# Row sums in another PSUM ring, one cast on another engine, and weight loads issued later, in a windowed attention kernel with a two-layer feed-forward behind it

## The chip, the cores and the metric

The kernel runs on one core of a Trainium2 chip. The metric is the device time of one execution in microseconds (us). Before the change the median of three runs is 311.28 us (310.89 to 311.34). A difference of less than about 0.2% is not told apart from none.

## What is computed

The reference is attention in a sliding window, followed by a feed-forward with a leaky ReLU. With q, k and v of shape (8 batches, 8 heads, 576 tokens, 64):

```python
scores = scale * np.matmul(q, k.transpose(0, 1, 3, 2))
mask = np.abs(pos[:, None] - pos[None, :]) <= 32
attn = softmax(np.where(mask, scores, -1e9))
x = np.matmul(attn, v)          # then to (4608 tokens, 512)
h = x @ w_in                    # 512 x 2048
out = np.maximum(0.01 * h, h) @ w_out   # 2048 x 512
```

All arrays are float32; the kernel works in bfloat16 with float32 sums.

## The kernel before, in words

**Units of work.** Two heads make a pair, so each batch has four pairs. For the first two batches one *item* is one pair and one half of the 576 tokens (288): items 0 to 3 are the four pairs of the first half of batch 0, items 4 to 7 those of its second half, items 8 to 15 belong to batch 1. Later batches use a different form (`score_blocks`, `product_blocks`, lines 363 to 406), which the change does not touch. "The second and third pairs" of the change are items 1 and 2.

**What an item needs, in order.** q and k of the pair are loaded by SP (`load_qk`, line 68) and v by GpSimd's own DMA queue, which also casts it (`load_cast_v`, line 143). q and k are cast to bfloat16 (`cast_qk`, line 265), transposed on TensorE into a PSUM buffer and copied out by ScalarE (`transposes`, line 306: a generator, of which each `next(first)` does q or k of one pair). Then:

- `score` (408): ten small matmuls into the one score buffer `ps` (419), the exponential on ScalarE (431), the product with the 0/1 mask on GpSimd (433; item 0's on VectorE), which gives `prob`;
- `row_sums` (446): two matmuls of `prob` with a block of ones (454) into PSUM, which spread each row's sum over the partitions;
- `inverse` (460): a reciprocal of these sums on VectorE (462); `sums` (465) does both;
- `product` (470): five matmuls with v into PSUM (477), and `scaled` (489): VectorE multiplies by the reciprocal and writes the item's part of `xT`, the input of the feed-forward.

**The feed-forward.** `xT` is multiplied with `w_in` in tiles of 128 hidden columns (`h_mms` 512, `h_tile` 525, index `f` from 0 to 15), ScalarE applies the leaky ReLU into `gT` (523), and `gT` is multiplied with `w_out` (585, 601). The first four hidden tiles of the first half are opened together by `h_first` (561), which goes through the four 128-row chunks of `xT` (one per pair, so one per item) and does all four tiles of a chunk before the next: four matmuls per `next(h0)`.

**PSUM.** There are eight banks: `ps` takes two, the pool `xps` has one buffer each for the names `s` (row sums) and `x` (products), and the pool `mmps` has four buffers that are handed out in turn to everything with the tag `mm`: the transposes of batch 0, the hidden tiles and the output tiles. Whoever takes a buffer waits until its former reader is done. So with the single buffer `s`, the row sums of an item wait until the reciprocal of the item before has read it.

**Order.** The kernel is scheduled by hand: each engine runs its instructions in the order in which the program issues them. Lines 688 to 750 write out the start (items 0 to 6 and the first hidden tiles); then the loop in line 764 runs the hidden tiles 4 to 15 of the first half, and `second_half` (754) does one more product, row sum and score between them. `warm_up` (610) and `keep_busy` (617) are matmuls without use for the result, with which TensorE is kept at work.

**Queues.** `load_w_in` (673) and `load_w_out` (676) load the weights in four parts each, 512 hidden columns at a time, and cast them; they are issued by GpSimd, between its mask products, and go through the software DMA queue. The q and k loads of batch 1 (line 740) are issued by SP, but a small memset on GpSimd (line 75), placed in GpSimd's order, has to run first. They feed the casts of batch 1 (784, 786, 778, 805), of which the last query cast is the one of pair 3.

**Later.** From group 2 on, a planner (810 to 837) spreads the steps of the other items between hidden and output tiles by due times. The change does not touch it.

Of the kernel before, what the change touches and what calls it, by code (L numbers as in the profile page):

```python
# [9 lines left out]
FP32 = mybir.dt.float32  # L10
# [6 lines left out]
def kernel(  # L17
# [15 lines left out]
    nc = tc.nc  # L33
# [9 lines left out]
    HALF = S // 2  # L43
# [14 lines left out]
    mmps = ctx.enter_context(tc.tile_pool(name="mmps", bufs=4, space=PS))  # L58
    scps = ctx.enter_context(tc.tile_pool(name="scps", bufs=1, space=PS))
    xps = ctx.enter_context(tc.tile_pool(name="xps", bufs=1, space=PS))  # L60
# [7 lines left out]
    def load_qk(b, p, behind=None):  # L68

        for into, src, name in ((qf, q, "qf"), (kf, k, "kf")):
            t = fload.tile([128, 2 * RUN * D], FP32, name=f"{name}{p}")
            if behind is not None:
                behind.memset(t[0:1, 0:1], 0.0)
                behind = None
            heads = src[b, 2 * p:2 * p + 2]
            if b == 0:

                into[b, p] = t[:, 0:NB * D]  # L80
                nc.sync.dma_start(  # L81
                    out=into[b, p], in_=heads.rearrange("a (p c) d -> (a p) (c d)", c=NB))
                continue
            t = t[0:96].rearrange("p (a r) -> p a r", a=2)
            if b < BY_DMA:
                nc.sync.dma_start(out=t, in_=heads.rearrange("a (p c) d -> p a (c d)", c=RUN))
            elif into is qf:
                nc.sync.dma_start(
                    out=t.rearrange("p a (g e) -> p a g e", g=3),
                    in_=heads.rearrange("a (g p c) d -> p a g (c d)", g=3, c=2),  # L90
                )
            else:
                nc.sync.dma_start(
                    out=t.rearrange("p a (c d) -> p a c d", d=D),
                    in_=heads.rearrange("a (c p) d -> p a c d", p=96),
                )
            into[b, p] = t
# [45 lines left out]
    def load_cast_v(b, p, heads=range(2)):  # L143

        for a in heads:
            r = slice(64 * a, 64 * a + 64)
            nc.gpsimd.dma_start(
                out=vbd[b % 2][r, p, :, r],
                in_=v[b, 2 * p + a].rearrange("(c p) d -> p c d", p=64),
            )  # L150
# [114 lines left out]
    def cast_qk(b, p, q_eng=nc.gpsimd, k_eng=nc.gpsimd):  # L265
        for eng, src, dst in ((q_eng, qf, qb), (k_eng, kf, kb)):
            if eng is None:
                continue
            if b == 0:
                to, tok = dst[:, p, 0:NB * D], src[b, p]  # L270
            else:
                to = dst[0:96, p].rearrange("p (c a d) -> p c a d", a=2, d=D)
                tok = src[b, p].rearrange("p a (c d) -> p c a d", d=D)
            if eng is nc.scalar:
                eng.activation(out=to, in_=tok, func=AF.Copy)
            else:
                eng.tensor_copy(out=to, in_=tok)  # L277
# [77 lines left out]
    def where(i):  # L355
        return i // 8, (i // 4) % 2, i % 4
# [6 lines left out]
    def score_blocks(i):  # L363
        p, bs = i % NPAIR, blocks_of(i)
        n = 2 * 64 * len(bs)
        lo = 512 * (i % 2)
        sc = ps[:, lo:lo + n].rearrange("p (a w c i) -> p a w c i", a=2, c=2, i=32)
        for w, (b, m) in enumerate(bs):
            tok = qz[b % 2][:, p, m // 3].rearrange("p a (c i) -> p a c i", c=2)
            at = 32 * (m % 3)  # L370
            nc.tensor.matmul(  # L371
                sc[:, :, w], kz[b % 2][:, p, 64 * m:64 * m + 128],
                tok[:, :, :, at:at + 32], start=True, stop=True,
            )
        e = attn.tile([128, 2 * HALF], BF16, name="e")
        nc.scalar.activation(out=e[:, 0:n], in_=ps[:, lo:lo + n], func=AF.Exp, scale=scale)  # L376
        pr = prob[:, i % NPROB].rearrange("p n i -> p (n i)")[:, 0:n]
        nc.gpsimd.tensor_mul(pr, e[:, 0:n], band.rearrange("p w c i -> p (w c i)")[:, 0:n])  # L378
        probs[i] = pr.rearrange("p (a w i) -> p a w i", a=2, i=64)
# [28 lines left out]
    def score(i, masked_by=nc.gpsimd):  # L408
        if i >= OLD:
            return score_blocks(i)  # L410
        b, hf, p = where(i)
        tok = qT[b][:, p, hf * HALF:hf * HALF + HALF]
        if b == 0:

            for a, n_, m in ((0, 0, 0), (1, 1, 0), (0, 0, 1), (1, 1, 1), (0, 0, 2),
                             (0, 1, 0), (1, 0, 0), (0, 1, 1), (1, 0, 1), (1, 0, 2)):
                blk, i0, n = WIN[hf][n_][m]
                r = slice(64 * a, 64 * a + 64)
                nc.tensor.matmul(  # L419
                    ps_v[r, n_, i0:i0 + n], first_keys[p][r, 64 * blk:64 * blk + 64],  # L420
                    tok[r, i0:i0 + n], start=True, stop=True,
                )
        else:
            for n_, blocks in enumerate(WIN[hf]):
                for blk, i0, n in blocks:
                    nc.tensor.matmul(  # L426
                        ps_v[:, n_, i0:i0 + n], kbd[b % 2][:, p, blk],
                        tok[:, i0:i0 + n], start=True, stop=True,
                    )
        e = attn.tile([128, 2 * HALF], BF16, name="e")  # L430
        nc.scalar.activation(out=e, in_=ps[:, P0:P0 + 2 * HALF], func=AF.Exp, scale=scale)  # L431
        pr = prob[:, i % NPROB]
        masked_by.tensor_mul(  # L433
            pr.rearrange("p n i -> p (n i)"), e, mask[hf].rearrange("p n i -> p (n i)"),
        )
        probs[i] = [pr, None, None]
# [9 lines left out]
    def row_sums(i):  # L446

        pr, both, _ = probs[i]
        s = xps.tile([128, 512], FP32, name="s")[:, 0:HALF]
        if both is not None:  # L450
            nc.tensor.matmul(s, ones_bd, both, start=True, stop=True)
        else:
            for n in range(2):
                nc.tensor.matmul(  # L454
                    s, ones_bd, pr[:, n],
                    start=(n == 0), stop=(n == 1),
                )
        probs[i][2] = s

    def inverse(i):  # L460
        r = recip.tile([128, HALF], FP32, name="r")
        nc.vector.reciprocal(r, probs[i][2])  # L462
        probs[i][2] = r

    def sums(i):
        if probs[i][2] is None:
            row_sums(i)
            inverse(i)
# [20 lines left out]
    def scaled(i):  # L489
        _, x, r = probs.pop(i)  # L490
        nc.vector.tensor_mul(place(i), x, r)  # L491
# [118 lines left out]
    def warm_up(n):  # L610
        t = xps.tile([128, 512], FP32, name="x")
        for _ in range(n):
            nc.tensor.matmul(
                t[:, 0:128], ones_bd, ones_bd, start=True, stop=True, skip_group_check=True,
            )
# [57 lines left out]
    def load_w_in(f0, f1):  # L673
        nc.gpsimd.dma_start(out=w_in_bf[:, :, f0:f1], in_=w_in_r[:, :, f0:f1])

    def load_w_out(i):
        c = slice(4 * i, 4 * i + 4)
        nc.gpsimd.dma_start(out=w_out_bf[:, c, :], in_=w_out_r[:, c, :])

    first = transposes(0)  # L680

    def clear_on_act(t):
        nc.scalar.activation(
            out=t.rearrange("p n j -> p (n j)"),
            in_=zero.to_broadcast([128, NB * 128]), func=AF.Copy,
        )
# [16 lines left out]
    load_cast_v(0, 3, (0,))  # L703
    cast_qk(0, 2, nc.vector, nc.vector)
    score(1)
    sums(0)
    cast_qk(0, 3, None, nc.gpsimd)
    next(first)
    next(first)
    cast_qk(0, 3, nc.scalar, None)  # L710
    warm_up(4)
    load_w_in(512, 1024)
    sums(1)
    score(2)
    load_cast_v(0, 3, (1,))
    load_w_in(1024, 1536)
    next(first)
    next(first)
    product(0)
    scaled(0)  # L720
    score(3)
    sums(2)
    product(1)
    scaled(1)
# [1 line left out]
    score(4)  # L726
    load_w_in(1536, 2048)
    clear_on_act(kbd[1][:, 1])
    load_w_out(0)
    h0 = h_first(0)  # L730
    h = next(h0)
    keep_busy(h, HALF, 3)
# [6 lines left out]
    clear_on_act(kbd[1][:, 2])  # L739
    for p in range(NPAIR):  # L740
        load_qk(1, p, nc.gpsimd if p == 0 else None)
    load_w_out(1)
    row_sums(4)
    product(3)
    scaled(3)
# [8 lines left out]
    def second_half():  # L754

        i = state["done"]
        weighted(i)
        if i < 7:
            sums(i + 1)
        if i < 5:  # L760
            score(i + 3)
        state["done"] += 1

    for f in range(4, FFC):
        h_tile(0, f)
        if f in (4, 8, 12):
            second_half()
        if f == 4:
            load_w_out(3)
            for t in (vbd[1][:, 0], vbd[1][:, 1], kbd[1][:, 3]):  # L770
                nc.gpsimd.memset(t, 0.0)
# [142 lines left out]
```

## Time and profile before

| | |
|---|---|
| median of three runs | 311.28 us (310.89 to 311.34) |
| the profiled execution: its own time, and its span | 311.33 us, 309.6 us |
| TensorE matmuls (PE) | 296.8 us busy, 96% |
| VectorE (DVE) | 223.9 us, 72% |
| ScalarE (ACT) | 203.8 us, 66% |
| GpSimd (POOL) | 200.9 us, 65% |
| matmuls of the first layer, line 515 | 956, 133.1 us |
| matmuls of the second layer, line 585 | 537, 122.5 us |
| row-sum reciprocals, line 462 | 16, 1951 ns each |
| mask products on GpSimd, line 433 | 15, 1297 ns each |

The span runs from the first to the last instruction on the core; the execution's own time is 1.7 us longer. Times in the profile are counted from the start of the span. "PE" is TensorE's matmuls, "PEld" its weight loads, "SPq" SP's DMA issues. A line of the timeline gives start, duration, engine, line of the kernel, operation, output and input, how many instructions were merged, and in brackets how long the engine had been idle and what released it. A line of the chain gives start, duration and the work that the end was waiting for. The profile prints the clock granted to TensorE as 1.00 in every stretch.

### The profile page before, as it was taken

How to read it: one execution, taken by the hardware profiler on the slowest of the kernel's cores; microseconds unless marked ns; L12 is line 12 of the kernel's file. 1: busy time of each engine (PE TensorE's matmuls, PEld its weight loads, DVE VectorE, ACT ScalarE, POOL GpSimd, SP SyncE). 2: the span in 40 equal slices, each digit the busy share in tenths (PEclk: the TensorE clock that was granted, in tenths of full speed). 3: DMA queues.
4: the chain of work that ended last, by engine and by line, in shares of the span. 5: the costliest groups of instructions: out<-in, count | busy, mean ns of one | idle time of the engine just before them, and what ended most of it. 6: DMA issues, size and time to landing. Idle time of an engine off the chain costs nothing.

```text
span 309.6 us, 6903 instructions
## 1 busy us (share of the span) xinstructions
PE 296.8 (96%) x2601; PEld 194.2 (63%) x2630; DVE 223.9 (72%) x300; ACT 203.8 (66%) x421; POOL 200.9 (65%) x254
## 2 busy tenths in 40 slices
PE   2889999999999999999999999999999999999996
PEld 2657865585856768685858585959555555444643
DVE  5778679798879987898799777898679866744000
ACT  6657784482965858585849584849588548842731
POOL 8798699959799997779579357578857522110000
PEclk9999999999999999999999999999999999999999
DMA  7999999997999899999999998895960110001002
GB/s 242 201 153 215 267 215 174 253 177 169 217 217 197 194 240 162 209 151 253 186 172 166 244 224 127 188 206 102 209 129 1 37 68 36 0 34 70 35 27 75
DMA packets 121505, 48.29 MB, mean 156 GB/s; under 512 B 96256, under 2 KB 115968, under 8 KB 121472
## 3 DMA queue, kind: packets, MB, share of 16 engines
q1 hardware_dynamic: 107776, 42.48, 67.2%
q0 software_dynamic: 13696, 5.38, 14.8%
q8 instruction: 20, 0.33, 0.5%
q14 instruction: 13, 0.11, 0.1%
HBM read 36.70 MB, written 9.44 MB: 149 GB/s over the span
## 4 chain that ended last, share of the span: by engine, by line
PE 83%; DMA 8%; DVE 4%; issue 1%; ACT 1%; POOL 0%; SPq 0%; ACTq 0%; DVEq 0%
PE mm L585 37%; PE mm L515 35%; DMA kf<-in_k_dram 6%; PE ps L371 4%; DVE r L462 3%; DMA set<-in_v_dram 2%; PE s L389 2%; PE x L389 2%; PE s L454 1%; PE ps L419 1%; PE x L477 1%; SPq L81 0%; ACT kT L331 0%; PE ps L426 0%; DVE xT L491 0%
## 5 line engine op out<-in xcount | busy, mean ns | idle before, releaser
L515 PE MATMUL mm<-xT,w_in_bf 128*128 128x256 bf16 (+3 forms) x956 | 133.1, 294 | 0.2
L585 PE MATMUL mm<-w_out_bf,gT 128*128 128x512 bf16 (+2 forms) x537 | 122.5, 373 | 1.3
L398 DVE RECIPROCAL r<-r 128x256 f32<-128x256 f32 (+1 forms) x56 | 95.0, 1696 | 35.5 <-ACT r L397 35.1
L515 PEld LDWEIGHTS <-w_in_bf 128*128 128x128 bf16 x960 | 91.5, 98 | 29.9 <-issue 0.2
L378 POOL TENSOR_TENSOR prob<-e,band 128x512 bf16<-128x512 bf16 (+1 forms) x56 | 62.6, 1117 | 57.5 <-ACT e L376 56.5
L585 PEld LDWEIGHTS <-gT 128*128 128x128 bf16 x560 | 52.1, 98 | 54.1
L523 ACT ACTIVATE gT<-mm 128x288 bf16<-128x288 f32 (+2 forms) x112 | 50.0, 478 | 11.8 <-PE mm L515 8.9
L376 ACT ACTIVATE e<-ps 128x512 bf16<-128x512 f32 (+1 forms) x56 | 32.4, 579 | 27.6 <-PE ps L371 26.2
L590 ACT ACTIVATE o_sb<-mm 128x512 f32<-128x512 f32 (+2 forms) x35 | 20.5, 585 | 39.3 <-PE mm L585 39.1
L546 ACT ACTIVATE gT<-mm 128x512 bf16<-128x512 f32 x64 | 35.7, 596 | 5.3 <-PE mm L515 3.9
L462 DVE RECIPROCAL r<-s 128x288 f32<-128x288 f32 x16 | 31.2, 1951 | 5.0 <-PE s L454 3.0
L402 DVE TENSOR_TENSOR xT<-x,r 64x256 bf16<-64x256 f32 (+1 forms) x56 | 24.4, 435 | 3.3
L402 DVE TENSOR_TENSOR xT<-s,r 64x256 bf16<-64x256 f32 (+1 forms) x56 | 24.4, 435 | 3.3
L277 POOL CAST kb<-kf 96x768 bf16<-96x768 f32 (+1 forms) x29 | 23.8, 820 | 3.7 <-DMA kf<-in_k_dram 3.6
L433 POOL TENSOR_TENSOR prob<-e,mask 128x576 bf16<-128x576 bf16 x15 | 19.4, 1297 | 5.2 <-ACT e L431 4.2
L371 PEld LDWEIGHTS <-set 128*128 128x128 bf16 x216 | 16.8, 98 | 9.3
L303 DVE COPY set<-kT 64x576 bf16<-64x576 bf16 x48 | 21.4, 446 | 0.9
L371 PE MATMUL ps<-set 128*128 128x128 bf16 x216 | 21.2, 219 | 0.0
L277 POOL CAST qb<-qf 96x768 bf16<-96x768 f32 x24 | 19.7, 819 | 0.2 <-DMA qf<-in_q_dram 0.2
L282 POOL CAST set<-vbuf 128x640 bf16<-128x640 f32 x24 | 17.2, 716 | 4.0 <-DVE r L398 2.0
L389 PEld LDWEIGHTS <-set 128*128 128x128 bf16 x432 | 18.0, 98 | 0.5
L283 POOL CAST set<-vbuf 64x512 bf16<-64x512 f32 x24 | 14.7, 610 | 1.5
(91 smaller groups left out, 235.7 us busy)
## 6 DMA issues: line engine op xcount, KB each, us to landing
qf<-in_q_dram SPq DMA_DIRECT2D x32, 288.0 KB, 5.7
kf<-in_k_dram SPq DMA_DIRECT2D x32, 288.0 KB, 6.2
out_dram<-o_sb SPq DMA_DIRECT2D x35, 256.0 KB, 2.5
vbuf<-in_v_dram SPq DMA_DIRECT2D x15, 256.0 KB, 4.9
w_in_bf<-in_moe_w_in_dram POOLq DMA_DIRECT2D x4, 512.0 KB, 7.2
w_out_bf<-in_moe_w_out_dram POOLq DMA_DIRECT2D x4, 512.0 KB, 14.6
vbuf<-in_v_dram SPq DMA_DIRECT2D x10, 192.0 KB, 4.3
set<-in_v_dram POOLq DMA_DIRECT2D x16, 72.0 KB, 6.0
```

The lines of the kernel that those rows point to most:

```text
L277: eng.tensor_copy(out=to, in_=tok)
L371: nc.tensor.matmul(sc[:, :, w], kz[b % 2][:, p, 64 * m:64 * m + 128], tok[:, :, :, at:at + 32], start=True, stop=True,)
L376: nc.scalar.activation(out=e[:, 0:n], in_=ps[:, lo:lo + n], func=AF.Exp, scale=scale)
L378: nc.gpsimd.tensor_mul(pr, e[:, 0:n], band.rearrange("p w c i -> p (w c i)")[:, 0:n])
L389: nc.tensor.matmul(x[:, a, w], vw[b % 2][:, p, m, a:a + 2].rearrange("p n d -> p (n d)"), pr[:, a, w], start=True, stop=True,)
L398: nc.vector.reciprocal(r[:, 0:n], r[:, 0:n])
L402: nc.vector.tensor_mul(xT[rows, p, t0:t0 + n].rearrange("p (w i c) -> p w c i", i=32, c=2), x[rows, a].rearrange("p (w c i) -> p w c i", c ...
L462: nc.vector.reciprocal(r, probs[i][2])
L515: nc.tensor.matmul(h[:, 0:n], w_in_bf[:, c, ts(f, 128)], xT[:, c, t0:t0 + n], start=(c == 0), stop=(c == DMC - 1),)
L523: nc.scalar.activation(out=to, in_=h, func=AF.Prelu, alpha=0.01)
L546: nc.scalar.activation(out=gT[:, f - 1:f + 1, t0:t0 + 256], in_=hh.rearrange("p (f t) -> p f t", f=2), func=AF.Prelu, alpha=0.01,)
L585: nc.tensor.matmul(o[:, lo:hi], gT[:, f, t0:t0 + 128], w_out_bf[:, f, lo:hi], start=(f == 0), stop=(f == FFC - 1),)
```

## The change

Four things change, all in the first 60 us:

- `row_sums` puts the sums of items 1 and 2 in buffers of the `mm` ring; the others stay in `s`.
- The queries of the fourth pair (pair 3 of batch 0) are cast by VectorE, right behind the casts of the third pair, and no more by ScalarE; the call stands before `sums(0)`. Its keys are still cast by GpSimd. The fourth pair's queries are then transposed before the warm-up matmuls and the row sums of item 1, its keys after the scores of item 2.
- `load_w_in(1024, 1536)` moves behind the scores of item 3, so behind its mask product on GpSimd, and `load_w_out(0)` behind the q and k loads of batch 1.
- The second and third `second_half` steps come one hidden tile sooner, after f = 7 and f = 11.

```diff
     def row_sums(i):
         pr, both, _ = probs[i]
-        s = xps.tile([128, 512], FP32, name="s")[:, 0:HALF]
+        if i in (1, 2):
+            s = mmps.tile([128, 512], FP32, name="mm", tag="mm")[:, 0:HALF]
+        else:
+            s = xps.tile([128, 512], FP32, name="s")[:, 0:HALF]
...
     score(1)
+    cast_qk(0, 3, nc.vector, nc.gpsimd)
     sums(0)
-    cast_qk(0, 3, None, nc.gpsimd)
     next(first)
     next(first)
-    cast_qk(0, 3, nc.scalar, None)
+    next(first)
     warm_up(4)
     load_w_in(512, 1024)
     sums(1)
     score(2)
     load_cast_v(0, 3, (1,))
-    load_w_in(1024, 1536)
-    next(first)
     next(first)
     product(0)
     scaled(0)
     score(3)
+    load_w_in(1024, 1536)
     sums(2)
...
     load_w_in(1536, 2048)
     clear_on_act(kbd[1][:, 1])
-    load_w_out(0)
     h0 = h_first(0)
...
         load_qk(1, p, nc.gpsimd if p == 0 else None)
+    load_w_out(0)
     load_w_out(1)
...
         h_tile(0, f)
-        if f in (4, 8, 12):
+        if f in (4, 7, 11):
             second_half()
```

## The prediction

> **What bounds the kernel now.** I read the page's first two parts (busy shares, the forty slices), then the chain that ended last in order of time, then the timeline of the first 60 us engine by engine, then the DMA issues of that stretch with their landings. TensorE is busy 296.8 of 309.6 us. The slices say where it is not: the first three and the last.
>
> ```profile
> span 309.6 us, 6903 instructions
> ...
> PE   2889999999999999999999999999999999999996
> ```
>
> From 24 us on TensorE is nearly the whole chain: in the timeline its matmuls follow each other at 0.123 us (128x288), 0.216 us (128x512), and only a few gaps are left. What can be won lies ahead of 24 us, and in the gap at 52 us. The chain there:
>
> ```profile
> 10.98 1.97 DVE r L462
> 13.00 0.66 PE s L454 x2
> 13.66 0.62 PE ps L419 x10
> ...
> 16.75 0.61 PE s L454 x2
> 17.38 1.97 DVE r L462
> 19.40 0.43 PE s L454 x2
> 19.86 1.97 DVE r L462
> 21.87 0.42 PE s L454 x2
> ...
> 25.07 12.02 DMA kf<-in_k_dram
> ...
> 50.41 1.88 DVE r L462
> 52.34 0.42 PE s L454 x2
> ```
>
> Up to 25 us it is a ladder of reciprocal, row sum, reciprocal: the row sums share one buffer `s`, so those of item 1 (13.00) start when the reciprocal of item 0 has read it (10.98 + 1.97), those of item 3 (19.40) when that of item 2 has. Read the first column down: 17.38, 19.86 are the rungs that the change can move. Then the chain leaves TensorE for the q and k loads of the second batch and returns to it at 52.34, where one wait is left:
>
> ```profile
> 42.39 1.60 DVE L277 CAST qb<-qf 96x768 bf16<-96x768 f32 x1 [0.88 <-DMA qf<-in_q_dram]
> ...
> 52.33 0.11 PEld L454 LDWEIGHTS <-ones_bd 128*128 128x128 bf16 x2 [0.60 <-DVE r L462]
> ```
>
> The four 128x512 matmuls before it start at 51.20, so TensorE is free at 51.20 + 4 x 0.216 = 52.06 and loses 0.28. VectorE has worked without a pause worth naming from 42.39, when the last queries of batch 1 landed, to 52.28. So a TensorE that comes earlier to 52 us wins nothing unless these loads come earlier too. That couples two parts of the change.
>
> **Part 1: row sums of items 1 and 2 in `mm` banks, fourth queries cast on DVE.** Starts are from the timeline, steps are differences of starts there. TensorE's order becomes: transposes q2 (10.88), k2 (11.38), q3 (+0.50: 11.88; its cast goes 10.10 to 10.56 on DVE, behind the cast that began at 9.64, and its load landed 3.63 + 6.3 = 9.9), four warm-up matmuls (+0.59: 12.47), row sums 1 (+0.43: 12.90; mask product 1 ends 12.46), scores 2 (+0.59: 13.49), transposes k3 (+0.45: 13.94), product 0. Row sums 1 gain only 0.10: TensorE's own queue takes the place of the wait.
>
> The gain is one rung later. Scores 3 stood at 16.09 behind two ScalarE copies after exp 2 (q3, k3); q3's copy now runs ahead of exp 2. Exp 2 14.20 to 14.85, copy of k3 14.75 to 15.41, scores 3 at 15.46. Mask product 2 on GpSimd follows exp 2 by 0.09 and takes 1.26: it ends 16.20, so row sums 2 start at 16.26, not 16.68. From there to the reciprocal it was 0.70 (16.68 to 17.38) while matmuls ran slowly, and 0.46 (19.40 to 19.86) once fast. Reciprocal 2 therefore starts at 16.96 or 16.72.
>
> A wait is added. Buffers of `mm` go round: row sums 1 and 2 take the fourth and second, so the fourth hidden tile of `h_first` falls on that of row sums 2 and its first matmul waits for reciprocal 2; row sums 3 stand behind it in TensorE's order. Before, they waited for the same reciprocal, so the price is one matmul, 0.12. Rung: reciprocal 2 ends 18.92 (18.68), + 0.06 + 0.12 + 0.46: reciprocal 3 at 19.56 (19.32) against 19.86. **Gain 0.30, or 0.54** if matmuls are fast by 16.3. The later rungs are unchanged and carry it to 25 us.
>
> Which? No column shows the step (the granted clock is printed 1.00 throughout), but the durations do: a pair of row sums took 0.66 at 16.68 and 0.42 at 19.40, ten score matmuls 0.66 at 16.09 and 0.43 at 18.00. So the step is near 17.7, some 4.7 us after the last wait above 0.4 us that TensorE had (12.58 to 13.00). That wait goes, and work without such a pause now begins at 10.88: by the same 4.7 us the step falls at 15.6, ahead of row sums 2. I take 0.54.
>
> The Trainium skill, TensorE: Matmul & The Clock Gate, Part 1 on the HAM clock gate, says that the clock is doubled after one busy window of about 3.4 us and that this window runs free of the kernel. Counted back from 17.7, windows would end at 14.3 and 10.9, and 14.3 gives the same sum; but if the window of 10.9 to 14.3 still counts as idle, the step stays at 17.7, which is the first rival below. No run here shows the window itself.
>
> Unseen costs: the reciprocal from an `mm` bank (1.88 to 1.97 from `s`: 1.96 taken, plus or minus 0.1 each); the DVE cast (0.45 to 0.65 in its three like rows, 1.60 at worst in the row above). Even 1.60 would end at 11.70, reciprocal 0 at 13.66, while reciprocal 1 is ready at 13.60: nothing. The ScalarE cast that goes (0.68 at 12.69) lay beside other work: nothing by itself. The cast of the fourth keys keeps its place: GpSimd's order of instructions lists it behind mask product 1 in both kernels.
>
> **Part 2: weight loads behind the mask products, `load_w_out(0)` behind the q and k loads.** GpSimd issues each in 0.75 to 0.81:
>
> ```profile
> 21.29 0.75 POOL L678 DMA_DIRECT2D w_out_bf<-in_moe_w_out_dram  x1
> 22.05 1.29 POOL L433 TENSOR_TENSOR prob<-e,mask 128x576 bf16<-128x576 bf16 x1
> 23.27 0.09 POOL L75 MEMSET qf<- 1x1 f32 x1
> ```
>
> The marker memset releases SP's eight loads (23.39). New GpSimd times: mask product 2 ends 16.20, v issue to 17.0, product 3 to 18.27, w_in issue to 19.06, product 4 to 20.33, w_in issue to 21.14. Exp 5 ended at 21.72 and comes 0.54 earlier, 21.18; product 5 21.27 to 22.56 without the w_out issue ahead of it; memset 22.49; SP at 22.61. **The loads are issued 0.78 earlier** (0.54 with the smaller gain). The weights do not suffer: w_in's third part waited in its queue anyway (issued 17.05, landed 24.1; the part before landed at 19.7), and so w_out(0) (issued 21.29, landed 32.4, first used at 42.1).
>
> Does an earlier issue land earlier? The first load took 7.0 us, the last 17.1, and from 23.7 to 27.2 only software-queue packets moved: the loads wait behind weights already queued. Ends: 0 and 0.88 (VectorE's idle time before the 42.39 cast). With less queued ahead I take the full 0.78.
>
> **Part 3: second-half steps after f = 7 and 11, not 8 and 12.** Four matmuls, 0.49, move behind each of the two steps. Counted on the old clock, row sums 6 stood ready at 27.93; now TensorE reaches them at 27.40, and reciprocal 5 (25.45 + 1.96) lets them go at 27.47. Row sums 7 follow reciprocal 6: 0.15 of waiting, where 30.32 to 30.51 held 0.14. Cost 0.08 in all. VectorE ends its reciprocals 0.4 earlier, but nothing on TensorE waited for that: the last product stays at 32.2.
>
> **Sum.** TensorE would be ready for the row sums of 52.34 at 52.06 - 0.54 + 0.08 = 51.60; VectorE lets them go at 52.34 - 0.78 = 51.56. So 51.60, **0.74 earlier**. Behind that the matmuls show no further wait on a load with a fixed time, and the tail is the same work. The profiled run took 311.33 (span 309.6): 310.59. The median, 311.28, is 0.05 lower; I forecast **310.6 us**.
>
> **Rivals.**
>
> *The step to fast matmuls stays at 17.7.* For it: gaps of 0.1 to 0.3 remain between the small matmuls. Against: the 0.42 pause is gone. Gain 0.30, loads 0.54 earlier: TensorE 52.06 - 0.30 + 0.08 = 51.84, VectorE 51.80. Time 311.33 - 0.50 = 310.8.
>
> *The q and k loads do not come earlier*, so that part 2 does not do what it says. For it: both queues are full from 27.4 to 42, and the loads land 1.6 to 3 us apart whatever their issue. Against: the first began only 3.5 us after its issue, and fewer weights are now queued ahead. Then the row sums of 52.34 wait as before and TensorE's gain is lost there: 311.3.
>
> *Slower: the last part of w_in lands too late.* It is issued at 20.33 and landed at 28.04; f = 12 needed it at 29.65. Now f = 12 starts at 30.28 - 0.54 = 29.74. If the q and k packets, now ahead of w_out(0), take its turns, it may land as late as the next weight load did before, 32.4: TensorE waits 32.4 - 29.74 = 2.7, less the 0.74: 311.33 + 1.9 = 313.2. It decides from a landing after 29.7. Against: q and k packets have moved with the weights at about equal counts, which doubles at most the last engine's remaining work.
>
> **Chances.** Forecast case 0.50 (its own range, from plus or minus 0.1 on two reciprocals, an end at 0.88 for the loads and the small waits of 22 to 31 us: 310.2 to 310.8); step stays 0.22; loads stay 0.16; w_in late 0.08; other mishaps on the slow side 0.04. A measurement of this kernel tells about 0.2% (0.62 us, so below 310.66 or above 311.90) from no change. Of the forecast case 0.42 falls below 310.66 and 0.08 within, of the second 0.06 and 0.16, of the third 0.13 within and 0.03 above. Faster 0.48, same 0.37, slower 0.15. The range leaves out the late weights and half of the slower rest: 309.9 (all waits of 22 to 31 us gone as well, another 0.6) to 311.5.
>
> **What would show it.** Right: row sums 1 near 12.9, row sums 2 near 16.3 with 0.42 and not 0.66; reciprocal 3 near 19.3; SP's first load of batch 1 near 22.6; the cast of 42.39 near 41.6; the row sums of 52.34 near 51.6 without a 0.28 wait. Wrong: ten score matmuls at 0.66 after 16 us, that cast still at 42.4, or a TensorE wait at f = 12.

## The result, and the profile after

The changed kernel takes 310.34 us (median of 22 runs, 309.62 to 311.59); the kernel before took 311.50 us beside it (22 runs, 310.43 to 313.6). The ratio is 0.9962, with a 95% interval of 0.9948 to 0.9975: 1.2 us less, between 0.8 and 1.6. The forecast was 310.6 us, 0.7 us less.

The profiled execution of the changed kernel took 311.11 us. Its page:

```profile
span 309.4 us, 6903 instructions
...
PE   2879999999999999999999999999999999999996
```

All slices but the third (7, where it was 8) have the digits of before: the change is too small for them. The start shows it, where row sums and reciprocals release each other like the rungs of a ladder. This is the chain that leads to 53 us, in order of time (start, duration, work):

```profile
13.39 0.48 PE mm L458 x2
...
16.56 0.42 PE mm L458 x2
17.00 1.97 DVE r L466
19.01 0.28 PE mm L519
19.29 0.26 PE s L458 x2
19.58 1.97 DVE r L466
21.59 0.42 PE s L458 x2
...
51.08 0.86 PE mm L589 x4
51.95 0.27 PE s L458 x2
```

Read it against the chain of before. Row sums 2 start at 16.56 and, at 0.42, are fast; reciprocal 3 starts at 19.58. Between them stands the new wait that the prediction had put down: a hidden-tile matmul (19.01) that waits for the reciprocal ending at 18.97, and row sums 3 behind it. And the chain no longer leaves TensorE for the q and k loads: the row sums of 52 us follow the matmuls ahead of them.

In this execution the loads at the very start landed later (the second pair's queries at 6.95, not 6.40), which shifts the ladder by 0.3 us; TensorE's instructions up to there are the same. So the table counts its times from a common point, the first transpose of the third pair's queries, taken as reciprocal 0 less 0.11: 10.87 us before, 11.19 after. Where the text takes a value from the table it is on this common clock; all other times are counted from the start of the span.

| profile of | step to fast matmuls | reciprocal 3 | SP's first load of batch 1 | row sums of 52 us | later waits of TensorE over 0.25 | last matmul |
|---|---|---|---|---|---|---|
| before | 6.8 | 8.98 | 12.52 | 41.46 | 0.27 just ahead | 295.66 |
| before, again | 5.6 | 8.76 | 12.38 | 41.25 | 0.27 just ahead | 295.44 |
| changed | 4.2 | 8.38 | 11.62 | 40.60 | 0.30 at 87 us | 295.09 |
| changed, again | 2.7 | 8.17 | 11.40 | 40.79 | 0.41 at 43, 0.38 at 87 | 295.37 |
| changed, third | 5.2 | 8.39 | 11.62 | 40.61 | none | 294.81 |
| part 1 alone | 4.9 | 8.65 | 12.23 | 41.20 | 0.33 just ahead | 295.39 |
| loads alone | 3.7 | 8.50 | 11.95 | 40.72 | none | 294.92 |
| old steps | 3.3 | 8.39 | 11.63 | 40.61 | 0.42 at 88 | 295.22 |
| item 1 only | 3.7 | 8.28 | 11.57 | 40.50 | 0.32 at 83, 0.64 at 88 | 295.65 |
| w_out alone | 3.2 | 8.77 | 12.01 | 41.00 | none | 295.19 |
| early warm-up | -4.1 | 7.20 | 10.44 | 39.42 | 1.39 at 100 | 295.01 |
| v sooner | 2.1 | 7.96 | 11.19 | 40.18 | 0.88 at 130 | 295.33 |
| warm-up, v sooner | -3.0 | 7.25 | 10.49 | 39.81 | none | 294.00 |
| item 1, v sooner | 3.2 | 8.27 | 11.56 | 40.50 | none | 294.70 |

All columns but the second and sixth are starts in the timelines. A wait is the time from one matmul's start to the next beyond the columns of the first at 2.4 per ns (the rate that 0.216 us for 512 columns gives, but for 3 ns). The step is where the trace's clock record begins to grant the full clock; in "w_out alone" and "item 1, v sooner" it has no such record, and the step is read from the durations.

What became of the time after 52 us is shown by GpSimd. This is its third v cast of batch 2, before (times from the start of the span, idle time and releaser in brackets):

```profile
79.90 0.72 POOL L282 CAST set<-vbuf 128x640 bf16<-128x640 f32 x1 [2.04 <-DVE r L398]
```

and after:

```profile
79.79 0.72 POOL L282 CAST set<-vbuf 128x640 bf16<-128x640 f32 x1 [1.75 <-DMA vbuf<-in_v_dram]
```

The cast comes at nearly the same time in both, though TensorE was 0.54 ahead at 52 us. Its load sets that time, to within 0.15: it landed at 79.75 before, a little ahead of the VectorE work that released the cast there, and at 79.64 after. (In the second profile of before the load released the cast too, at 80.03.) From this cast on GpSimd works almost without a pause up to a mask product that ends at 87.94 before and at 87.84 after, and TensorE's product behind it started at 88.14 before. So TensorE had 0.20 to spare there, 0.14 in the second profile of before, and a gain of 0.54 is more than that. In TensorE's weight loads after, the lack shows as a pause of 0.25 ahead of the product:

```profile
87.54 0.10 PEld L389 LDWEIGHTS <-set 128*128 128x128 bf16 x1
87.89 0.27 PEld L389 LDWEIGHTS <-set 128*128 128x128 bf16 x7 [0.25 <-issue]
```

### The profile page after: what moved, and what is told of

The parts are those of the page before. It is cut to its first block, busy times and chain, and to the rows that moved or that the text cites. A ratio compares the mean times of both kernels' runs of the same rounds, so it can differ in the third digit from the quotient of the medians.

```text
span 309.4 us, 6903 instructions
## 1 busy us (share of the span) xinstructions
PE 295.8 (96%) x2601; PEld 194.0 (63%) x2630; DVE 222.6 (72%) x301; ACT 203.3 (66%) x420; POOL 201.0 (65%) x254
## 4 chain that ended last, share of the span: by engine, by line
PE 84%; POOL 4%; DMA 4%; SPq 2%; DVE 2%; ACT 2%; issue 1%; POOLq 0%; ACTq 0%
PE mm L519 35%; PE mm L589 35%; PE ps L371 3%; DMA vbuf<-in_v_dram 2%; PE mm L605 2%; PE s L389 2%; PE x L389 2%; DMA qf<-in_q_dram 2%; SPq L112 1%; DVE r L466 1%; POOL prob L378 1%; PE s L458 1%; POOL prob L433 1%; PE tp L319 1%; PE x L481 1%
## 5 line engine op out<-in xcount | busy, mean ns | idle before, releaser
L466 DVE RECIPROCAL r<-s 128x288 f32<-128x288 f32 x14 | 27.3, 1951 | 3.0 <-PE s L455 2.4
L371 PEld LDWEIGHTS <-set 128*128 128x128 bf16 x216 | 16.8, 98 | 9.2
```

The source lines that it names most:

```text
L371: nc.tensor.matmul(sc[:, :, w], kz[b % 2][:, p, 64 * m:64 * m + 128], tok[:, :, :, at:at + 32], start=True, stop=True,)
```

## The experiments

The theory at the outset was that the ladder and the loads are coupled, because the row sums of 52 us wait for whichever of TensorE and the q and k loads comes later, so that a ladder alone or loads alone gain little. Its rivals were that one of the two parts is all of it. Ratios are to the kernel before, with 95% intervals.

### Part 1 alone, and part 2 alone

Part 1 alone is the kernel before with

```diff
-        s = xps.tile([128, 512], FP32, name="s")[:, 0:HALF]
+        if i in (1, 2):
+            s = mmps.tile([128, 512], FP32, name="mm", tag="mm")[:, 0:HALF]
+        else:
+            s = xps.tile([128, 512], FP32, name="s")[:, 0:HALF]
...
     score(1)
+    cast_qk(0, 3, nc.vector, nc.gpsimd)
     sums(0)
-    cast_qk(0, 3, None, nc.gpsimd)
     next(first)
     next(first)
-    cast_qk(0, 3, nc.scalar, None)
+    next(first)
     warm_up(4)
...
     load_w_in(1024, 1536)
     next(first)
-    next(first)
```

and neither weight load moved. The loads alone are the kernel before with

```diff
-    load_w_in(1024, 1536)
     next(first)
     next(first)
...
     score(3)
+    load_w_in(1024, 1536)
...
-    load_w_out(0)
     h0 = h_first(0)
...
         load_qk(1, p, nc.gpsimd if p == 0 else None)
+    load_w_out(0)
```

> Part 1 alone: row sums of items 1 and 2 in mm buffers, fourth queries cast on VectorE; loads and steps as before. Times are counted from the first transpose of the third pair's queries (10.88 in the profile before, 11.20 in that after), since the loads ahead of it land 0.3 us apart. Theory (ladder and loads are coupled): reciprocal 3 starts 8.4 later, as after (before 8.98); but w_out(0) is still issued ahead of mask product 5, so SP's first load of batch 1 starts near 12.4 (before 12.51, after 11.61), and TensorE gives most of the ladder's gain back at the row sums that stand at 52.34 before: 41.3 (before 41.46, after 40.60), with a wait of about 0.6 there. Time within 0.1% of before, about 0.1 to 0.2 us less. Rival (the ladder alone is the gain): these row sums at 40.8 without that wait, time 0.2 to 0.4% less, as the whole change.

Measured, part 1 alone: 0.9979 (0.9966 to 0.9993). SP's load at 12.23 and the row sums at 41.20 with a wait of 0.33, not 0.6: the gain is held there as the theory has it, but less of it. The time, 0.21% less, is more than the theory's 0.1% and no less than the rival's 0.2%; the interval takes in both. Reciprocal 3 started at 8.65, not 8.4, and the reason is in GpSimd's timeline:

```profile
15.25 1.26 POOL L433 TENSOR_TENSOR prob<-e,mask 128x576 bf16<-128x576 bf16 x1 [1.06 <-ACT e L431]
16.46 0.80 POOL L147 DMA_DIRECT2D set<-in_v_dram  x1
17.25 0.79 POOL L677 DMA_DIRECT2D w_in_bf<-in_moe_w_in_dram  x1
18.06 2.51 POOL L433 TENSOR_TENSOR prob<-e,mask 128x576 bf16<-128x576 bf16 x2
```

and in TensorE's of the same kernel:

```profile
19.01 0.28 PE L518 MATMUL mm<-xT,w_in_bf 128*128 128x288 bf16 x1 [0.31 <-DVE r L465]
19.40 0.41 PE L457 MATMUL s<-prob,ones_bd 128*128 128x288 bf16 x2
```

The v issue and the weight issue stand ahead of mask product 3, which ends near 19.3; row sums 3 start at 19.40 for its sake and not at 19.13 behind the hidden-tile matmul. So the move of `load_w_in(1024, 1536)` is itself a part of the ladder, 0.27 of it. The prediction had the new GpSimd times right but saw in this move only the loads.

> Part 2 alone: the w_in part behind the scores of item 3 and w_out(0) behind the q and k loads of batch 1; row sums, casts and steps as before. Theory: reciprocal 3 at 9.0 after the first transpose of the third pair's queries, as before; mask product 5 no longer stands behind a weight issue, SP's first load at 12.2 to 12.3 (before 12.51), the last query cast of batch 1 some 0.25 earlier, and the wait of 0.28 at the row sums of 52.34 all but gone: 41.2 (before 41.46, after 40.60). Time about 0.25 us less, 0.999. Rival (the order of the loads is the gain, the rest beside the point): 40.6 there and 0.996 to 0.997 in time. Second rival (weights late): a wait at f = 8 or f = 12, slower.

Measured, loads alone: 0.9988 (0.9972 to 1.0003). The time is the theory's 0.999, but the profile came near the rival's 40.6 for the row sums: 40.72, and no wait. Reciprocal 3 came at 8.50, not 9.0. A part of this is the w_in issue that no longer holds mask product 3: "w_out alone" below, which leaves it in its place, has 8.77. The rest is outside the change. TensorE's timeline:

```profile
12.58 0.66 PE L454 MATMUL s<-prob,ones_bd 128*128 128x288 bf16 x2 [0.41 <-DVE r L462]
...
15.68 0.43 PE L419 MATMUL ps<-set,kT 64*64 64x96 bf16 x10 [0.73 <-ACT kT L331]
16.04 0.42 PE L454 MATMUL s<-prob,ones_bd 128*128 128x288 bf16 x2
```

The pause of 0.41 ahead of row sums 1 is still there, and yet scores 3 and row sums 2 are fast, 0.43 and 0.42 where the first profile of before shows 0.66 for each. The step to fast matmuls fell at 14.2 us, not 17.6. It came 1.6 us after the end of that pause, which contradicts the prediction's rule that the step comes 4.7 us after the last long pause.

Added up, the two parts' times, 0.21% and 0.12% less, make 0.33%, and the whole change has 0.35 to 0.38%. The intervals are too wide (0.14% and more to each side) to tell this sum from a coupled one.

### The old steps, and only item 1 in an mm buffer

Both are the changed kernel with one edit. The old steps:

```diff
-        if f in (4, 7, 11):
+        if f in (4, 8, 12):
```

and item 1 only:

```diff
-        if i in (1, 2):
+        if i in (1,):
```

> The whole change but for the steps, which stay after f = 8 and 12. Theory: part 3 costs 0.08 us on TensorE or nothing, so this is the changed kernel within 0.1%: reciprocal 3 at 8.4, SP's first load at 11.6, the row sums of 52.34 at 40.5 to 40.6, counted from the first transpose of the third pair's queries; 0.996 to 0.998 of before. Rival (earlier steps free VectorE for the casts of batch 1, and that is what shortens 52 us): the last query cast and these row sums come 0.3 to 0.4 later than in the changed kernel, time 0.1% more than it.

Measured: 0.9968 (0.9955 to 0.9981), and every column of the table up to 52 us as in the changed kernel (8.39, 11.63, 40.61). Part 3 is worth nothing that shows; its VectorE work does come earlier (reciprocal 7 at 19.02 with the change and 19.50 without), and nobody waits for it.

> The whole change, but only the row sums of item 1 go to an mm buffer; those of item 2 stay in s, whose former reader, reciprocal 0, ends before they start. Theory: row sums 3 then wait for reciprocal 2 directly and not behind a hidden-tile matmul that waits for it: reciprocal 3 at 8.26 after the first transpose of the third pair's queries (after 8.38, before 8.98), the row sums of 52.34 at 40.5; time 0.1 us less than the changed kernel, not to be told from it. Rival (both must leave s): reciprocal 3 at 8.9, time as before.

Measured: reciprocal 3 at 8.28, row sums at 40.50: 0.10 sooner, as the theory had it, so the new wait behind the hidden-tile matmul costs what was put down for it. But the profile then lost 0.96 in two waits near 83 and 88 us, and the time is 0.9975 (0.9962 to 0.9987), no better than the change.

### The same kernels once more

> The kernel before, profiled once more. The step to fast matmuls stood at 17.6 in its first profile, and at 15.4, 16.1, 14.2, 14.5 and 14.9 in those of the changed kernel and four variants, one of them (loads alone) with the pause of 0.42 us still ahead of it. Theory now (the step falls anywhere within some 3.4 us, whatever the pauses): it need not be at 17.6 again; where it is below 16 us, reciprocal 3 starts 8.7 to 8.8 after the first transpose of the third pair's queries (8.98 with the late step), bounded by mask product 3, which waits for the w_in issue. Rival (the pause of 12.58 to 13.00 delays the step): 17.3 to 17.9 again and 8.98.

Measured (one execution, 311.44 us): the step at 16.8 us, 5.6 in the table, and reciprocal 3 at 8.76. The rival's 17.3 to 17.9 did not come. Reciprocal 3 is where the theory had it for a step below 16, though the step was not quite so early.

> The changed kernel, profiled once more. Its first profile gained 0.86 up to the row sums that stood at 52.34 (counted from the first transpose of the third pair's queries) and lost 0.30 of it near 87.5 us, where a product waited for a mask product behind v loads. Theory (the ladder is fixed by the order, the v loads' landing is not): reciprocal 3 at 8.4 and these row sums at 40.6 again, the later wait anywhere from 0 to 1.0. Rival (the later wait is the price of coming earlier): 0.3 again within 0.05.

Measured (one execution, 310.88 us): reciprocal 3 at 8.17, earlier than expected, since the step fell at 2.7, ahead of scores 2 too. The row sums came at 40.79, because of a wait (0.41 as the table counts it) that the first profile had not:

```profile
43.44 1.89 PE L605 MATMUL mm<-w_out_bf,gT 128*128 128x512 bf16 x8 [0.24 <-DMA w_out_bf<-in_moe_w_out_dram]
```

The third part of w_out landed at 43.4 (before: 41.9 in the first profile, 40.8 in the second; first profile after: 43.1), and TensorE, earlier, was there ahead of it. This is the price of the later w_out issue: the same part landed at 41.4 in part 1 alone, which does not move w_out, and at 43.1 in "w_out alone", which moves nothing else. The wait near 87 us was 0.38.

> The changed kernel a third time, beside the three variants on the same chip. It gained 0.86 and 0.67 up to the row sums of 52.34 in its two profiles (counted from reciprocal 0), lost 0.30 and 0.38 of it near 87 us, where a product waits behind v loads, and 0.41 at 43 us in the second, where an output matmul waited for the third part of w_out. Theory (these waits come from loads that land at fixed times): a wait of 0.2 to 0.6 near 87 us again, one at 43 us where that part lands after 43.3; time 0.996 to 0.998 of before. Rival (chance events of two profiles): no such waits.

Measured: 0.9965 (0.9950 to 0.9980), which repeats the result; in the profile neither wait. All its loads were early: the second pair's keys at 6.7 us (7.7 in the first profile after), the third part of w_out at 41.8, and the third v cast of batch 2 at 77.8, though still released by its load. TensorE was early as well, by 1.06 at the common point; against it w_out's part came 0.25 sooner than in the first profile after and the v cast 0.93. So the rival is not refuted: whether TensorE waits for these loads differs from one execution to the next.

### w_out alone

```diff
-    load_w_out(0)
     h0 = h_first(0)
...
         load_qk(1, p, nc.gpsimd if p == 0 else None)
+    load_w_out(0)
```

> The kernel before with one line moved: w_out(0) behind the q and k loads of batch 1. Loads alone had gained 0.74 up to the row sums of 52.34 in its profile. Theory (the w_in issue ahead of mask product 3 holds the ladder at reciprocal 3, the w_out issue ahead of mask product 5 holds SP's loads): reciprocal 3 at 8.7 to 9.0 after the first transpose of the third pair's queries, SP's first load 0.25 earlier than before in relation to it, the wait of 0.28 down to below 0.1, row sums at 41.1 to 41.25; time 0.2 to 0.3 us less than before. Rival (w_out alone is what loads alone gained): 40.7.

Measured: 0.9996 (0.9979 to 1.0013), no difference that can be told, where 0.2 to 0.3 us less was expected; the profile does show the effect. Reciprocal 3 at 8.77, the wait gone, the row sums at 41.00. SP's load comes 0.37 to 0.51 earlier than in the two profiles of before. The loads gain more than that: q and k packets begin to move 2.1 us after SP's first issue, against 3.9 and 3.7 in the profiles of before, and the last queries land at 40.9 us, against 42.4, although the ladder of this execution began 0.17 to 0.46 later. With one weight load less ahead of them, the loads wait less.

### Early warm-up, and sooner v loads

If the step and the v loads are what is left, each can be moved.

All are edits of the changed kernel. The early warm-up adds 32 matmuls of the kernel's own warm-up between the first steps:

```diff
+    warm_up(12)
     next(first)
     next(first)
+    warm_up(9)
...
+    warm_up(3)
     next(first)
+    warm_up(8)
```

The sooner v loads are due one item earlier:

```diff
-v_next = {OLD - 4: [(BY_DMA, 2, 2)]}
+v_next = {OLD - 5: [(BY_DMA, 2, 2)]}
```

"Warm-up, v sooner" has both of these edits, and "item 1, v sooner" the sooner v loads with the edit of item 1 only.

> The changed kernel with 32 more warm-up matmuls of 128x128 between the first transposes (12 ahead of them, 9 behind the first keys, 3 behind the first scores, 8 behind the second keys), so that TensorE has next to no pause from 3 us on. Theory (the step needs some 3.4 us of work and can be had earlier): matmuls are fast from 6.5 to 10 us on, the row sums, scores and transposes up to 16 us take two thirds of their time, reciprocal 3 starts 0.3 to 0.6 earlier in relation to the landing of the second pair's keys, and the time is 0.3 to 0.8 us less than that of the changed kernel. Rival (what lies ahead of 16 us waits for loads, casts and copies, not for matmuls): reciprocal 3 as in the changed kernel within 0.15, no difference in time, or slower by the warm-up matmuls that stand ahead of transposes.

Measured: the step at 7.0 us, reciprocal 3 at 7.20, 1.2 sooner than in the changed kernel, more than expected; the row sums of 52 us at 39.42. And of all this nothing that can be told is left in time: 0.9967 (0.9954 to 0.9980). In the profile one wait took 1.39:

```profile
100.50 0.91 DVE L303 COPY set<-kT 64x576 bf16<-64x576 bf16 x2 [2.54 <-DMA kT<-qb]
```

TensorE's scores near 100 us need queries that VectorE copies into place, which come by a transposing load. The expectation of 0.3 to 0.8 us less was wrong: what the start gains is not what the end sees.

> The changed kernel with one number more: the v loads of batch 2's last two pairs are issued at step 11, not 12, so SP takes them ahead of two transposing loads and an output store that wait for TensorE's work. Theory (the wait near 87 us is the lateness of these v loads): they land 3 us earlier, GpSimd no longer waits for them, the wait near 87 us is below 0.1, and the time is 0.2 to 0.4 us less than that of the changed kernel. Rival (GpSimd's own work holds that mask product): wait and time stay.

Measured: the third v cast at 77.08, 2.7 sooner than in the first profile after and without a wait; no wait near 87 us. But the time is 0.9968 (0.9956 to 0.9980), beside 0.9965 for the changed kernel on the same chip, and the profile shows 0.88 of waiting at 130 us, for another transposing load. The mechanism was right and the gain was not: in this profile a later load took its turn.

> Early warm-up matmuls and the sooner v loads together. Early warm-up alone reached the row sums of 52.34 2.0 earlier than before, counted from reciprocal 0, and lost 1.39 of it in one wait near 100 us, behind GpSimd's queue, which had waited for the same v loads. Theory (the loads give the floor): with the loads sooner the wait near 100 us falls below 0.6 and the time is 0.5 to 1.0 us less than that of the changed kernel, 0.993 to 0.995 of before. Rival (GpSimd's work from 78 to 96 us is the floor): the wait stays above 1.0 and the time is that of early warm-up alone, 0.997.

Measured: no later wait at all in the profile, whose execution took 309.51 us, and the lowest median of all, 310.29 us; 0.9955 (0.9935 to 0.9975). That is not told apart from the changed kernel's 310.43 in the same set, and it lies above the expected 0.993 to 0.995.

> Only item 1's row sums in an mm buffer, with the sooner v loads. Item 1 alone started reciprocal 3 0.10 sooner than the changed kernel but lost 0.97 in waits near 83 and 88 us. Theory: those waits go with the loads, and the time is 0.3 to 0.5 us less than that of the changed kernel, about 0.995 of before. Rival (GpSimd's own work): as the changed kernel or slower.

Measured: no later wait in the profile, but 0.9973 (0.9954 to 0.9992). The gain of 0.3 to 0.5 us was not there. None of the variants beats the changed kernel by more than the noise.

## Why the prediction was right, point by point

**The ladder: right in size, and a step wrong in its reason.** 0.54 was forecast; reciprocal 3 gained 0.60 between the first two profiles and 0.59 between the second two. The rungs are as forecast: row sums 1 came 0.14 sooner (0.10 forecast) and row sums 2 0.45 (0.42). But the sum rests on the prediction's step that the last pause of 0.42 decides when matmuls become fast ("by the same 4.7 us the step falls at 15.6"). Such a fixed distance does not hold: with the pause in place the step was seen at 6.8, 5.6, 3.7 and 3.2 on the common clock, without it (and without early warm-up) from 2.1 to 5.2 in eight profiles. The place in one execution is chance, and the first profile of before, from which the prediction took its price, was the latest of all.

The clock records show where the chance comes in. The stretch at the full clock lasts 293.55, 296.96, 300.37 or 303.79 us in the twelve profiles that have a record, whole multiples (86 to 89) of 3.413. So the clock changes only at points 3.41 us apart, and these points lie elsewhere in each execution. In the 3.41 us between two such points that end at the step, TensorE was busy for 3.00 to 3.41 us in all twelve, as the profile counts busy time; in the stretches ahead of that, which brought no step, for 3.00 at most. A pause of 0.41 falls on this border. In the first profile of before the stretch from 10.81 to 14.23 us of the span holds it and brought no step (2.998 us busy); in loads alone that from 10.77 to 14.18 holds it and did (3.002). In "old steps" the stretch begins at nearly the same place of the work as in the first profile of before (0.10 ahead of the common point, there 0.06), has no pause, was busy throughout, and the step came at its end. So the order with the pause does hold the step back, by a whole stretch, when the stretches lie as they did there, and there the prediction's price is right: reciprocal 3 comes 0.59 sooner in "old steps".

The Trainium skill, TensorE: Matmul & The Clock Gate, Part 1 on the HAM clock gate, says that the window after which the clock is doubled lasts about 3.4 us and runs free of the kernel. The trace agrees: the points 3.41 us apart. The prediction quoted this rule but took its price from one place of the window, with a rival of 0.22 beside it; the rule should have been the main case, with the price of the step as a range.

The low end of that range is better seen between profiles with a step between 3.2 and 5.6: reciprocal 3 at 8.76 and 8.77 with the old order, 8.38, 8.39 and 8.39 with the new one, a gain of 0.38. So it is luck that the measured 0.60 and 0.59 lie so near 0.54: the first pair had a late step before, the second an early one (2.7) after. The one matmul of waiting (0.12 forecast) is shown by "item 1 only", 0.10. That `load_w_in` ahead of mask product 3 would hold the ladder, part 1 alone showed; the prediction's sum contained it without naming it. Part 1's ring and its cast were not run apart, so how the gain divides between them stays open, but for this: the buffer for item 2 brings none, since reciprocal 3 came sooner without it.

**The loads: right.** 0.78 earlier was forecast for SP's first load, 0.90 and 0.98 were measured. Whether they also land earlier was the second rival's question (no, at 0.16): on the common clock the last queries of batch 1 landed 1.37 earlier in the first pair of profiles and 0.54 earlier in the second. The direction came from the packets: q and k loads had waited behind weights already queued. The wait of 0.28 ahead of the row sums of 52 us is gone in every profile in which w_out moved, and there in every one in which it did not.

**The weights: nearly right.** The slower rival, the last part of w_in late at f = 12, was not seen. The third part of w_out came 1.2 later instead, and cost 0.41 in one of three profiles.

**The steps: right.** 0.08 or nothing was forecast, nothing was seen.

**What follows 52 us: wrong.** "Behind that the matmuls show no further wait on a load with a fixed time" failed in two of three profiles of the changed kernel: 0.30 and 0.38 went to the v loads of batch 2. The prediction looked for waits that were there before, not for loads with little to spare: before, the load of the cast at 79.90 had landed 0.15 ahead of it.

**The sum: the way and about the size.** 0.74 was forecast for 52 us; the profiles show 0.86, 0.46 and 0.64 against the profile of before with the same number or, for the third, the second. At the last matmul the three profiles after average 295.09 and the two before 295.55, 0.46 less. The timed runs show 1.2 (0.8 to 1.6), more than either. The profiled executions themselves took 311.33 and 311.44 before, 311.11, 310.88 and 309.73 after, 0.8 apart on average. Where the timed runs find the rest stays open: the landing of the first loads moves by over 1 us from profile to profile (the second pair's keys at 6.7 to 8.0 us), and the waits for later loads come and go, so a few profiles cannot settle some tenths.

## What to carry to other kernels

Before adding up gains of tenths at the start of a long kernel, follow the freed engine to the first transfer that is not driven by it: early warm-up matmuls won 1.2 us more at 52 us, and in the one profile of that kernel all of it was lost at 100 us. A small instruction queue such as GpSimd's, which issues loads between mask products, has two prices at once, the product that waits behind the issue and the load that waits behind the product; price both. And a duration that differs within a profile only because the clock had not risen yet is no property of the kernel: take a second profile, or a range, before a term is built on it.

## What the runs showed of the hardware that was not expected

- 32 more matmuls of 128x128 from 3 us on were followed by a raised TensorE clock at 7.0 and 7.7 us, against 13.0 to 17.6 us in the ten profiles without them whose clock record shows the step.
- Loads in SP's queue started late when weights stood in the software queue: 3.7 to 3.9 us after issue with w_out's first part ahead of them (three profiles), 2.1 to 3.4 us with it behind them (eleven profiles).
- TensorE's clock changed only at points 3.41 us apart, at other places in each execution. It rose at the end of the first stretch between two such points in which TensorE was busy for 3.00 us or more (twelve profiles, busy time as the profile counts it): 3.002 us brought the step in loads alone, 2.998 us did not in the first profile of before.
